# Starting the operands of the attention-weighted sums on 16-byte multiples, and taking half a batch's softmax sums from the exp instruction, in a clustered-attention and spatial-gating kernel

## The chip, the cores and the metric

The kernel runs on one core of a Trainium2 chip. Times are microseconds (us) of one execution on the device. The engines are named as the profile names them: PE (matrix multiply) with PEld (its loading of the stationary operand), DVE (vector), ACT (scalar), POOL (GpSimd) and SP, which here only issues DMAs.

## The reference

Four batches of eight heads, 768 positions, head dimension 64. Queries and keys only see each other where they fall to the same of 16 centroids.

```
q_assign = argmax(q_n @ c_n, axis=-1);  k_assign = argmax(k_n @ c_n, axis=-1)
mask = q_assign[:, :, :, None] == k_assign[:, :, None, :]
scores = where(mask, scale * q @ k.T, -1e9)
attn = exp(scores - max(scores));  attn = attn / (sum(attn) + 1e-9)
x = attn @ v                                  # then (B, S, H*D)
h = maximum(x @ w_in, 0);  u, v = h[..., :512], h[..., 512:]
v_n = (v - mean(v)) / sqrt(var(v) + 1e-6)
out = (u * (w_spatial @ v_n + b_spatial)) @ w_out
```

## The kernel before

Every fp32 operand of a large product is split into two fp16 parts, a high one and a low one; a product is three matmuls (high by high, high by low, low by high). Work is counted in pairs of heads, `n` from 0 to 15 (four pairs to a batch), and in units of one head, `(n, part)`. A sequence is `NT` = 6 blocks of 128 positions.

`prep(n)` loads and splits a pair, assigns clusters and fills `vhl`, the tile of the values: for each block `k` and head `h` a row of 64 high columns, one column of ones (column 64), one spare column and 64 low columns (`vh.t[:, k, h, 0:D + 1]` and `vh.t[:, k, h, D + 2:]`), 130 fp16 columns in all. `shifts(u)` finds an upper bound of each query's scores: PE products at L759, each reduced by DVE at L765 out of one of four PSUM buffers called `acc`, so that PE gets a buffer back when DVE has read it.

`attend(u)` has two forms. For twelve pairs keys stand on partitions: for each key block `k` scores by PE (L862, L864), exp on ACT (L872), high part on ACT (L876), low part on POOL (L877), and then the weighted sums on PE (L882): 18 matmuls, for each of six query blocks `j` one of 65 columns with the high values and the ones, one of 64 columns with the low values, one of 65 columns with the low weights. The column of ones makes the sum of the weights, so one head's result is 65 columns per query block in one `acc` buffer: `av.t[:, j * (D + 1):...]`. At `k` = 0 six more matmuls of 65 columns add a mean term. For the pairs in `ROWS` (9, 11, 13, 15, `attend_rows`) queries stand on partitions: the maximum by DVE (L820), exp (L823), high part (L825), low part (L826), a DMA transpose, and the same 18 matmuls per query block (L831), so that each exp instruction there holds the whole row of weights of 128 queries. `results` (L917 to L921) divides by the sums and writes the input of the second half.

`mlp(b)` is the second half for a batch, all in matmuls of 512 columns at L948. Its groups of six matmuls are put between the attention work of later batches; those of the last batch come at the end.

The order in which the program issues everything is written out by hand: `ORDER` is a list of the 3,164 numbers of the operations, in which the numbers are counted as the code creates them. Each engine works through its own operations in that order. A buffer of `acc` or `wk` is given, in that order, to the next who asks, the longest free one first.

## Time and profile before

| | us |
|---|---|
| median of 3 runs | 637.48 |
| lowest, highest | 636.87, 639.26 |
| the profiled execution | 635.84 |
| its span, first to last instruction | 634.1 |
| PE busy in it | 605.9 (96%) |
| DVE, ACT, POOL busy | 475.4, 439.0, 435.2 |

The profiled execution took 1.74 us more than its span, and 1.64 us less than the median. "Busy" of PE counts each matmul to its modelled end, so that overlapping matmuls are one stretch; how fast matmuls follow each other is read from the starts of rows in the timeline.

### The profile page before, as it was taken

The numbers are of one execution on the slowest core, as the hardware profiler recorded it, in microseconds if no ns is written. First come the engines' busy times: TensorE is split into PE (matmuls) and PEld (weight loads), VectorE is DVE, ScalarE is ACT, GpSimd is POOL, SyncE is SP. The second block draws the span as 40 slices with busy tenths as digits, with TensorE's granted clock in tenths as the row PEclk, the third lists the DMA queues.
The fourth block names the chain that finished last, engine by engine and source line by source line (L and its number), as shares of the span: only waits on it lengthen the run. The fifth ranks groups of instructions, "written<-read, shape, count | busy, mean of one in ns | idle before, by whom it ended". The sixth has DMA issues, their size and how long they took to land.

```text
span 634.1 us, 16399 instructions
## 1 busy us (share of the span) xinstructions
PE 605.9 (96%) x6573; PEld 363.6 (57%) x6573; DVE 475.4 (75%) x994; ACT 439.0 (69%) x674; POOL 435.2 (69%) x309
## 2 busy tenths in 40 slices
PE   3889999989999999999999999999999999999997
PEld 2537666666666667556555575575556655544443
DVE  7899999999999996877959678669798475143120
ACT  6768999999978889566477787878669964121102
POOL 2456889999789799566667787678769977223120
PEclk9969999999999999999999999999999999999999
DMA  6467865875565576728989779988996199513115
GB/s 211 135 171 162 170 150 134 174 181 147 125 154 112 115 172 97 146 67 161 180 144 192 181 126 182 184 166 144 166 167 123 38 151 154 113 22 101 33 30 153
DMA packets 174812, 87.73 MB, mean 138 GB/s; under 512 B 158448, under 2 KB 161552, under 8 KB 174736
## 3 DMA queue, kind: packets, MB, share of 16 engines
q1 hardware_dynamic: 171136, 80.40, 62.7%
q10 hardware_dynamic: 3600, 6.30, 2.9%
q8 instruction: 51, 0.84, 0.6%
q14 instruction: 25, 0.20, 0.1%
HBM read 27.63 MB, written 6.29 MB: 53 GB/s over the span
## 4 chain that ended last, share of the span: by engine, by line
PE 69%; DVE 17%; POOL 4%; DMA 4%; issue 3%; ACT 1%; SPq 0%; ACTq 0%; DVEq 0%; POOLq 0%
PE acc L948 39%; PE acc L882 7%; DVE nm L765 7%; PE acc L759 5%; PE sc L862 4%; PE sc L864 4%; PE acc L831 4%; POOL wk L877 3%; PE sc L817 2%; PE sc L815 2%; DMA wk<-wk 1%; DVE vhl L541 1%; DVE nq L820 1%; DVE wk L988 1%; DMA oht<-ohx 1%
## 5 line engine op out<-in xcount | busy, mean ns | idle before, releaser
L877 POOL TENSOR_TENSOR wk<-wk,wk 128x768 f16<-128x768 f32 x144 | 245.7, 1730 | 48.9 <-ACT wk L876 36.0
L765 DVE TENSOR_REDUCE nm<-acc 128x1 f32<-128x512 f32 (+1 forms) x216 | 138.8, 681 | 13.8 <-PE acc L759 12.7
L872 ACT ACTIVATE wk<-sc,plog 128x768 f32<-128x768 f32 x144 | 126.7, 899 | 24.0 <-PE sc L864 17.9
L948 PE MATMUL acc<-win,xT 128*128 128x512 f16 x576 | 134.9, 379 | 1.0 <-DVE u L1009 0.7
L876 ACT CAST wk<-wk 128x768 f16<-128x768 f32 x144 | 116.6, 829 | 5.5 <-PE acc L882 2.8
L948 PE MATMUL acc<-vn,wsp 128*128 128x512 f16 x432 | 101.2, 379 | 0.0
L826 POOL TENSOR_TENSOR wk<-wk,wk 128x768 f16<-128x768 f32 x48 | 80.1, 1678 | 26.2 <-ACT wk L825 24.1
L882 PEld LDWEIGHTS <-wk 128*128 128x128 f16 x2592 | 89.8, 97 | 12.0 <-POOL wk L877 1.6
L882 PE MATMUL acc<-vhl,wk 128*128 128x65 f16 (+1 forms) x2592 | 95.0, 193 | 1.3 <-POOL wk L877 1.3
L948 PEld LDWEIGHTS <-xT 128*128 128x128 f16 x576 | 55.0, 97 | 62.6 <-issue 1.5
L759 PE MATMUL acc<-hq 80*128 80x512 f16 (+1 forms) x288 | 78.6, 347 | 8.8 <-DVE nm L765 4.0
L862 PE MATMUL sc<-hq,lo 128*128 128x512 f16 (+1 forms) x288 | 72.4, 333 | 1.0 <-ACT wk L872 0.7
L864 PE MATMUL sc<-hq 81*128 81x512 f16 (+1 forms) x288 | 72.3, 332 | 0.0
L948 PE MATMUL acc<-wou,wk 128*128 128x512 f16 x288 | 67.2, 379 | 0.0
L948 PEld LDWEIGHTS <-wsp 128*128 128x128 f16 x432 | 41.2, 97 | 45.2 <-issue 0.2
L823 ACT ACTIVATE wk<-sc,nq 128x768 f32<-128x768 f32 x48 | 47.2, 990 | 26.0 <-DVE nq L822 21.4
L820 DVE TENSOR_REDUCE nq<-sc 128x1 f32<-128x768 f32 x48 | 45.6, 951 | 23.2 <-PE sc L817 18.9
L1011 POOL TENSOR_TENSOR wk<-u,wk 128x512 f16<-128x512 f32 x24 | 29.0, 1216 | 48.4 <-DVE wk L1010 28.5
L1009 DVE SCALAR_TENSOR_TENSOR u<-acc,bsp,u 128x512 f32<-128x512 f32 x24 | 17.9, 747 | 54.5 <-PE acc L948 54.5
L1019 ACT ACTIVATE wk<-acc 128x512 f32<-128x512 f32 x24 | 13.9, 595 | 46.9 <-PE acc L948 44.3
L948 PEld LDWEIGHTS <-wk 128*128 128x128 f16 x288 | 27.9, 97 | 32.2 <-issue 0.2
L759 PEld LDWEIGHTS <-hq 80*128 80x128 f16 x288 | 27.0, 101 | 31.9 <-issue 17.3
(143 smaller groups left out, 884.7 us busy)
## 6 DMA issues: line engine op xcount, KB each, us to landing
raw<-in_kqT_dram SPq DMA_DIRECT2D x15, 768.0 KB
wk<-in_vp_dram SPq DMA_DIRECT2D x16, 384.0 KB
out_dram<-wk ACTq DMA_DIRECT2D x24, 256.0 KB
hq<-hq SPq DMA_DIRECT2D x15, 384.0 KB
hq<-lo SPq DMA_DIRECT2D x15, 192.0 KB
lo<-hq SPq DMA_DIRECT2D x15, 192.0 KB
wraw<-in_wsT_dram SPq DMA_DIRECT2D x12, 192.0 KB
vn<-in_w_in_dram SPq DMA_DIRECT2D x4, 512.0 KB
```

The lines of the kernel that those rows point to most:

```text
L759: T.matmul(out=acc.t[:, i * w:(i + 1) * w], lhsT=hq.t[0:R_SH, 1, h, t * P:(t + 1) * P], rhs=hq.t[0:R_SH, 0, h, cs], start=i == 0, stop=i = ...
L765: V.tensor_reduce(out=cols(nm.t), in_=src, axis=AX.X, op=ALU.max, negate=True)
L820: o = op("DVE", lambda sc=sc, nq=nq: V.tensor_reduce(out=nq.t[:, 0:1], in_=sc.t[:, 0:S], axis=AX.X, op=ALU.max, negate=True), after=[o], u ...
L823: o = op("ACT", lambda sc=sc, p32=p32, nq=nq: A.activation(out=p32.t, in_=sc.t[:, 0:S], func=AF.Exp, bias=nq.t[:, 2:3], scale=nq.t[:, 1:2] ...
L826: o = op("POOL", lambda pt=pt, p32=p32: G_.tensor_tensor(out=pt.t[:, 1, :], in0=p32.t, in1=pt.t[:, 0, :], op=ALU.subtract), after=[o], use ...
L862: T.matmul(out=sc.t[:, c:c + cs.stop - cs.start], lhsT=lo.t[:, h, ks], rhs=hq.t[:, 2, h, cs], start=True, stop=False)
L864: T.matmul(out=sc.t[:, c:c + cs.stop - cs.start], lhsT=hq.t[0:R_E, 0, h, ks], rhs=hq.t[0:R_E, 1, h, cs], start=False, stop=True)
L872: A.activation(out=p32.t, in_=sc.t[:, 0:S], func=AF.Exp, bias=plog, scale=SC_UNIT)
L876: o = op("ACT", lambda pt=pt, p32=p32: A.copy(out=pt.t[:, 0, :], in_=p32.t), after=[o], use=[p32], new=[pt])
L877: o = op("POOL", lambda pt=pt, p32=p32: G_.tensor_tensor(out=pt.t[:, 1, :], in0=p32.t, in1=pt.t[:, 0, :], op=ALU.subtract), after=[o], use ...
L882: T.matmul(out=av.t[:, j * (D + 1):j * (D + 1) + w], lhsT=lhsT, rhs=rhs, skip_group_check=True, **f)
L948: T.matmul(out=acc.t, lhsT=lr[m][0], rhs=lr[m][1], start=(m == 0), stop=(m == n - 1))
```

## The change

The row of `vhl` grows from 130 to 136 columns (272 bytes), with the low values from column 72 on; a query block's result in `acc` takes 68 columns (272 bytes) and not 65. The small tiles `wh` and `wl` now share one. In `attend_rows` exp gives the sum of each row as a second output (`accum_out`) into a new small tile `rs`, the three matmuls per block have 64 columns each, and `results` reads `rs` where it read column 64 of `acc`. The other twelve pairs keep the column of ones. `ORDER` is another list of the same 3,164 numbers; no engine has more or fewer instructions.

```diff
+LO, V_COLS, AV_COLS = 72, 136, 68
 ORDER = [
...
-    vhl = [const.tile([P, NT, 2, 2 * D + 2], F16, name="vhl%d" % i) for i in range(V_BUFS)]
+    vhl = [const.tile([P, NT, 2, V_COLS], F16, name="vhl%d" % i) for i in range(V_BUFS)]
...
-    whs = [const.tile([2, 2, D + 2], F16, name="wh%d" % i) for i in range(2)]
-    wls = [const.tile([2, 2, D + 2], F16, name="wl%d" % i) for i in range(2)]
+    whl = [const.tile([34, 2, D + 2], F16, name="whl%d" % i) for i in range(2)]
+    whs = [x[0:2] for x in whl]
+    wls = [x[32:34] for x in whl]
...
+    r_rs = R(sm, "rs", [P, NT], F32, 2)
...
# attend_rows
-            o = op("ACT", lambda sc=sc, p32=p32, nq=nq: A.activation(out=p32.t, in_=sc.t[:, 0:S], func=AF.Exp, bias=nq.t[:, 2:3], scale=nq.t[:, 1:2]), after=[o], use=[sc, nq], new=[p32])
+            o = op("ACT", lambda sc=sc, p32=p32, nq=nq, t=t: A.activation(out=p32.t, in_=sc.t[:, 0:S], func=AF.Exp, bias=nq.t[:, 2:3], scale=nq.t[:, 1:2], accum_out=rs.t[:, t:t + 1]), after=[o], use=[sc, nq] + ([rs] if t else []), new=[p32] + ([] if t else [rs]))
...
-                    T.matmul(out=av.t[:, t * (D + 1):t * (D + 1) + w], lhsT=lhsT, rhs=rhs, skip_group_check=True, **f)
+                    T.matmul(out=av.t[:, t * AV_COLS:t * AV_COLS + w], lhsT=lhsT, rhs=rhs, skip_group_check=True, **f)
                 for k in range(NT):
-                    mm(D + 1, ptT.t[:, k], vh.t[:, k, h, 0:D + 1], start=t == 0 and k == 0, stop=False)
-                    mm(D, ptT.t[:, k], vh.t[:, k, h, D + 2:], start=False, stop=False)
-                    mm(D + 1, ptT.t[:, NT + k], vh.t[:, k, h, 0:D + 1], start=False, stop=t == NT - 1 and k == NT - 1)
+                    mm(D, ptT.t[:, k], vh.t[:, k, h, 0:D], start=t == 0 and k == 0, stop=False)
+                    mm(D, ptT.t[:, k], vh.t[:, k, h, LO:], start=False, stop=False)
+                    mm(D, ptT.t[:, NT + k], vh.t[:, k, h, 0:D], start=False, stop=t == NT - 1 and k == NT - 1)
...
# attend
                     mm(j, D + 1, pt.t[:, 0, js], vh.t[:, k, h, 0:D + 1], start=False, stop=False)
-                    mm(j, D, pt.t[:, 0, js], vh.t[:, k, h, D + 2:], start=False, stop=False)
+                    mm(j, D, pt.t[:, 0, js], vh.t[:, k, h, LO:], start=False, stop=False)
                     mm(j, D + 1, pt.t[:, 1, js], vh.t[:, k, h, 0:D + 1], start=False, stop=stop)
...
# results
-        a = op("DVE", lambda: V.tensor_scalar(out=rc.t, in0=avv()[:, :, D], scalar1=f, scalar2=1e-9 * 2.0 ** P_LOG * f, op0=ALU.mult, op1=ALU.add), after=[prev], use=[av], new=[rc])
+        a = op("DVE", lambda: V.tensor_scalar(out=rc.t, in0=rs.t if rs else avv()[:, :, D], scalar1=f, scalar2=1e-9 * 2.0 ** P_LOG * f, op0=ALU.mult, op1=ALU.add), after=[prev], use=[rs or av], new=[rc])
```

The new list moves operations by a few places nearly everywhere. Two places follow as the built programs have them; line numbers of the changed kernel are three higher than those of the kernel before.

The first is the start of the first batch's second half. On PE of the kernel before, the last scores ahead of it and its first matmul, which stands 3,389 rows into PE's list:

```order
L864 LDWEIGHTS hq
L864 MATMUL sc_127<-hq 128x512
L864 LDWEIGHTS hq
L864 MATMUL sc_127<-hq 128x256
L948 LDWEIGHTS xT_104
L948 MATMUL acc_128<-win,xT_104 128x512 [waits DVE_49]
```

In the changed kernel that matmul stands 3,409 rows in, behind weighted sums:

```order
L885 LDWEIGHTS wk_119
L885 MATMUL acc_128<-vhl_89,wk_119 128x64
L885 LDWEIGHTS wk_119
L885 MATMUL acc_128<-vhl_89,wk_119 128x65
L951 LDWEIGHTS xT_102
L951 MATMUL acc_129<-win,xT_102 128x512 [waits DVE_49]
```

It waits for an `acc` buffer that DVE has to read first. On DVE of the kernel before, the seven instructions up to the one that frees it (281 on DVE's list):

```order
L765 TENSOR_REDUCE nm_91<-acc_128 128x1
L765 TENSOR_REDUCE nm_91<-acc_131 128x1 [waits PE_49]
L776 TENSOR_REDUCE nl<-nm_92 128x6 [waits DVE_49]
L541 SCALAR_TENSOR_TENSOR vhl_90<-wk_109,vhl_90 128x12x64 [waits DMAHW0_49,Activation_49]
L486 TENSOR_SCALAR acc_130<-wou 128x512 [waits DMAHW1_49]
L471 SCALAR_TENSOR_TENSOR wsp<-wraw_124,wsp 128x384 [waits DMAHW3_49]
L765 TENSOR_REDUCE nm_92<-acc_128 128x1 [waits DVE_49,PE_49]
```

On DVE of the changed kernel, the seven up to the one that frees it there (280 on the list):

```order
L768 TENSOR_REDUCE nm_91<-acc_128 128x1 [waits PE_49]
L768 TENSOR_REDUCE nm_92<-acc_126 128x1 [waits DVE_49,PE_49]
L768 TENSOR_REDUCE nm_91<-acc_129 128x1
L768 TENSOR_REDUCE nm_92<-acc_126 128x2 [waits PE_49]
L768 TENSOR_REDUCE nm_91<-acc_128 128x1
L474 SCALAR_TENSOR_TENSOR wsp<-wraw_122,wsp 128x384 [waits DMAHW1_49]
L768 TENSOR_REDUCE nm_91<-acc_129 128x2 [waits PE_49]
```

The same kinds of work stand ahead in both: PE has 20 rows (ten matmuls with their loads) more ahead of the second half, DVE one row fewer.

The second place is on PE at the first weighted sums of a pair in `ROWS`. Before:

```order
L817 LDWEIGHTS hq
L817 MATMUL sc_127<-hq 128x256
L831 LDWEIGHTS wk_113 [waits DMAHW5_49]
L831 MATMUL acc_130<-vhl_90,wk_113 128x65 [waits Activation_49]
L831 LDWEIGHTS wk_113
L831 MATMUL acc_130<-vhl_90,wk_113 128x64
```

After, where a group of the second half stands ahead:

```order
L951 LDWEIGHTS xT_103
L951 MATMUL acc_126<-win,xT_103 128x512
L834 LDWEIGHTS wk_110 [waits DMAHW1_49]
L834 MATMUL acc_128<-vhl_90,wk_110 128x64 [waits Activation_49]
L834 LDWEIGHTS wk_110
L834 MATMUL acc_128<-vhl_90,wk_110 128x64
```

The number of matmuls and of loads is the same; 576 matmuls lose one column.

## Rows read from the trace of the kernel before

**Rows 1.** The page, parts 1 and 2: busy time of PE (share of the span, instructions), and the granted PE clock in 40 slices of 15.9 us, in tenths.

```profile
PE 605.9 (96%) x6573; PEld 363.6 (57%) x6573; DVE 475.4 (75%) x994; ACT 439.0 (69%) x674; POOL 435.2 (69%) x309
...
PEclk9969999999999999999999999999999999999999
```

**Rows 2.** Busy time by stretch of the span: from:to, length, then busy us and instructions of each engine, granted clock, DMA share, GB/s.

```profile
0.00:60.00 60.00, 44.90 (x417) 25.69 (x418) 54.38 (x137) 42.17 (x66) 28.75 (x34) 0.86 0.63 172
60.00:140.00 80.00, 74.20 (x1208) 53.77 (x1207) 78.19 (x154) 78.78 (x128) 74.45 (x49) 1.00 0.74 162
140.00:216.00 76.00, 74.08 (x972) 49.19 (x972) 73.26 (x147) 68.48 (x114) 64.72 (x43) 1.00 0.57 133
216.00:634.00 418.00, 412.74 (x3979) 234.96 (x3977) 269.55 (x559) 249.57 (x370) 267.32 (x186) 1.00 0.67 130
```

**Rows 3.** What PE waited for between 60 and 216 us: waiting line, whom for, us in total, times, longest.

```profile
PE acc L759 <- DVE nm L765: 3.3, 6, 1.0
PE acc L882 <- POOL wk L877: 1.3, 2, 1.0
PE acc L759 <- DMA hq<-oht: 0.9, 1, 0.9
```

**Rows 4.** The same between 216 and 634 us (two of four rows; the others are 0.2 us each).

```profile
PE acc L948 <- DVE u L1009: 0.7, 1, 0.7
PE acc L831 <- DMA wk<-wk: 0.4, 1, 0.4
```

**Rows 5.** The weighted sums of L882 by stretch: from:to, length, PE busy (number of matmuls), PEld busy, clock, DMA share, GB/s.

```profile
0.00:140.00 140.00, 33.76 (x912) 32.09 (x912) 0.94 0.69 166
140.00:216.00 76.00, 21.11 (x570) 20.28 (x570) 1.00 0.57 133
216.00:634.00 418.00, 44.49 (x1254) 43.13 (x1254) 1.00 0.67 130
```

**Rows 6.** The weighted sums of L831 (pairs in `ROWS`) in the last stretch; they have none in the others.

```profile
216.00:634.00 418.00, 32.88 (x864) 31.58 (x864) 1.00 0.67 130
```

**Rows 7.** PE's timeline at two long runs of weighted sums: start, us to the modelled end, line, number. The row behind each run shows where the next matmul starts.

```profile
239.52 3.47 PE L882 MATMUL acc<-vhl,wk 128*128 128x65 f16 x108
242.82 0.49 PE L862 MATMUL sc<-hq,lo 128*128 128x512 f16 x2
...
453.22 1.82 PE L831 MATMUL acc<-vhl,wk 128*128 128x65 f16 x54
454.87 0.49 PE L815 MATMUL sc<-lo,hq 128*128 128x512 f16 x2
```

**Rows 8.** PE's timeline in unit (4, 1), `h` = 1: the groups of 18 for key blocks `k` = 1, 2 and 5, each with the row that follows it.

```profile
157.08 0.70 PE L882 MATMUL acc<-vhl,wk 128*128 128x65 f16 x18
157.62 0.60 PE L759 MATMUL acc<-hq 80*128 80x256 f16 x3
...
158.93 0.71 PE L882 MATMUL acc<-vhl,wk 128*128 128x65 f16 x18
159.48 0.38 PE L759 MATMUL acc<-hq 80*128 80x512 f16 x1
...
163.74 0.70 PE L882 MATMUL acc<-vhl,wk 128*128 128x65 f16 x18
164.28 0.38 PE L759 MATMUL acc<-hq 80*128 80x256 f16 x2
```

**Rows 9.** PE's timeline at 24 matmuls of cluster logits, 64 and 32 columns by turns (L641, L642; first row and the row that follows the last), whose operands all start on multiples of 16 bytes.

```profile
228.60 0.19 PE L641 MATMUL sc<-cmx,hq 128*128 128x64 f16 x1
...
229.26 0.49 PE L862 MATMUL sc<-hq,lo 128*128 128x512 f16 x2
```

**Rows 10.** Groups of instructions: line, engine, operation, out<-in, shapes, number | busy us, mean ns | idle before, whom for.

```profile
L823 ACT ACTIVATE wk<-sc,nq 128x768 f32<-128x768 f32 x48 | 47.2, 990 | 26.0 <-DVE nq L822 21.4 <-issue 2.1 <-POOL wk L826 1.9
L872 ACT ACTIVATE wk<-sc,plog 128x768 f32<-128x768 f32 x144 | 126.7, 899 | 24.0 <-PE sc L864 17.9 <-DMA wk<-wk 3.2 <-POOL wk L877 2.3
L782 ACT ACTIVATE shx<-nl 128x6 f16<-128x6 f32 x24 | 5.5, 229 | 4.1 <-DVE nl L776 2.4 <-DMA sht<-shx 1.7
L541 DVE SCALAR_TENSOR_TENSOR lo<-raw,hq 128x768 f16<-128x768 f32 x28 | 32.4, 1166 | 3.1 <-ACT hq L613 2.8 <-ACT hq L552 0.3
L541 DVE SCALAR_TENSOR_TENSOR vhl<-wk,vhl 128x768 f16<-128x768 f32 x13 | 17.4, 1339 | 1.9 <-ACT vhl L693 1.9
```

**Rows 11.** The timeline of DVE and of PE around the start of the first batch's second half.

```profile
144.50 0.68 DVE L765 TENSOR_REDUCE nm<-acc 128x1 f32<-128x512 f32 x1
...
145.23 2.75 PE L948 MATMUL acc<-win,xT 128*128 128x512 f16 x12 [0.24 <-DVE nm L765]
```

**Rows 12.** The chain that ended last, its longest piece (start, us, what).

```profile
542.30 85.48 PE acc L948 x396
```

More of the change, by code (lines that the diff above doesn't have):

```diff
@@ L367 @@
     r_vhl = R(None, "vhl", None, None, V_BUFS, tiles=vhl)
-    r_vhl0 = R(None, "vhl0", None, None, 2, tiles=[wspf[:, 1560 * i:1560 * (i + 1)].rearrange("p (t h c) -> p t h c", t=NT, h=2) for i in range(2)])
+    r_vhl0 = R(None, "vhl0", None, None, 2, tiles=[wspf[:, 2 * NT * V_COLS * i:2 * NT * V_COLS * (i + 1)].rearrange("p (t h c) -> p t h c", t=NT, h=2) for i in range(2)])
     scratch = r_wk.new()
@@ L693, in values @@
         o_vh = op("ACT", lambda: A.activation(out=vh.t[:, :, :, 0:D], in_=vraw.t.rearrange("p t (h d) -> p t h d", d=D), func=AF.Copy, scale=V_SCALE), after=[ldv, c_one], use=[vraw], new=[vh])
-        o_vl = low(n, 2, lambda: vh.t[:, :, :, D + 2:], lambda: vraw.t.rearrange("p t (h d) -> p t h d", d=D), lambda: vh.t[:, :, :, 0:D], V_SCALE, [o_vh], [vraw, vh], [])
+        o_vl = low(n, 2, lambda: vh.t[:, :, :, LO:], lambda: vraw.t.rearrange("p t (h d) -> p t h d", d=D), lambda: vh.t[:, :, :, 0:D], V_SCALE, [o_vh], [vraw, vh], [])
         if n in ROWS:
@@ L704, in sums @@
                 T.matmul(out=o[:, :, 0:D + 1], lhsT=ones, rhs=vh.t[:, t, :, 0:D + 1], start=(t == 0), stop=False, skip_group_check=True)
-                T.matmul(out=o[:, :, 0:D], lhsT=ones, rhs=vh.t[:, t, :, D + 2:], start=False, stop=(t == NT - 1), skip_group_check=True)
+                T.matmul(out=o[:, :, 0:D], lhsT=ones, rhs=vh.t[:, t, :, LO:], start=False, stop=(t == NT - 1), skip_group_check=True)
         short = n >= 2 * NPR
@@ L806, in attend_rows @@
         hq, lo, vh = X["hq"], X["lo"], X["vhl"]
-        av = r_acc.new()
+        av, rs = r_acc.new(), r_rs.new()
         prev = None
@@ L830, in mm @@
                 def mm(w, lhsT, rhs, **f):
-                    T.matmul(out=av.t[:, t * (D + 1):t * (D + 1) + w], lhsT=lhsT, rhs=rhs, skip_group_check=True, **f)
+                    T.matmul(out=av.t[:, t * AV_COLS:t * AV_COLS + w], lhsT=lhsT, rhs=rhs, skip_group_check=True, **f)
                 for k in range(NT):
-                    mm(D + 1, ptT.t[:, k], vh.t[:, k, h, 0:D + 1], start=t == 0 and k == 0, stop=False)
-                    mm(D, ptT.t[:, k], vh.t[:, k, h, D + 2:], start=False, stop=False)
-                    mm(D + 1, ptT.t[:, NT + k], vh.t[:, k, h, 0:D + 1], start=False, stop=t == NT - 1 and k == NT - 1)
+                    mm(D, ptT.t[:, k], vh.t[:, k, h, 0:D], start=t == 0 and k == 0, stop=False)
+                    mm(D, ptT.t[:, k], vh.t[:, k, h, LO:], start=False, stop=False)
+                    mm(D, ptT.t[:, NT + k], vh.t[:, k, h, 0:D], start=False, stop=t == NT - 1 and k == NT - 1)
             prev = op("PE", values, after=[o, prev] + X["v"], use=[ptT, vh] + ([av] if t else []), new=[] if t else [av])
-        results(u, av, prev)
+        results(u, av, prev, rs)
     def attend(u):
@@ L881, in mm @@
                 def mm(j, w, lhsT, rhs, **f):
-                    T.matmul(out=av.t[:, j * (D + 1):j * (D + 1) + w], lhsT=lhsT, rhs=rhs, skip_group_check=True, **f)
+                    T.matmul(out=av.t[:, j * AV_COLS:j * AV_COLS + w], lhsT=lhsT, rhs=rhs, skip_group_check=True, **f)
                 for j, (h, t) in enumerate(u.blocks):
@@ L895, in attend, with results @@
         results(u, av, prev)
-    def results(u, av, prev):
+    def results(u, av, prev, rs=None):
         b, p = divmod(u.n, NPR)
@@ L906, in avv @@
         def avv():
-            return av.t[:, 0:NT * (D + 1)].rearrange("p (t c) -> p t c", c=D + 1)
+            return av.t[:, 0:NT * AV_COLS].rearrange("p (t c) -> p t c", c=AV_COLS)
         def dst(i):
```

264 rows, old and new, of the table ORDER are left out of this document.

## The prediction

> **What bounds the kernel now.** I read the page's busy times first, then the span in four stretches, then what PE waited for in each. PE is busy for 605.9 of 634.1 us, the other engines for 475 and less [rows 1]. The stretches tell when that holds. Up to 60 us PE has 44.9 us of work and DVE 54.4; the clock granted to PE is 0.86 on average and lowest in the third slice [rows 1, 2]. From 60 to 140 us DVE is busy for 78.2 of 80 us and ACT for 78.8: PE can only have what they hand over. From 140 to 216 us PE has 74.1 of 76 us and DVE 73.3, so both matter. From 216 us on PE has 412.7 of 418 us and DVE only 269.6 [rows 2].
>
> The waits agree. Up to 216 us the longest sum is PE waiting for DVE to read an `acc` buffer, 3.3 us in six waits [rows 3]; behind 216 us the two largest are single waits of 0.7 and 0.4 us [rows 4]. At the end the chain is one piece of 85.5 us of PE, 396 matmuls [rows 12]. So what PE is spared after 216 us should come off the time, what it is spared before 140 us should turn into waiting for DVE, and between the two I count half.
>
> **The weighted sums on PE.** Busy time doesn't price a matmul here, because matmuls overlap; the distance of starts does. In one run of 108 it is (242.82 - 239.52) / 108 = 30.6 ns, in one of 54 at L831 (454.87 - 453.22) / 54 = 30.6 ns [rows 7]. All attention-weighted sums cost that: 2,736 at L882, of which 912 up to 140 us, 570 from there to 216 us and 1,254 after it [rows 5], and 864 at L831, all after 216 us [rows 6].
>
> What would they cost with aligned operands? Three rows bound it. The stretch of 396 wide matmuls takes 215.9 ns for each, 2.5 ns over 512 columns at 2.4 GHz [rows 12]; with 65 and 64 columns that makes 29.6 and 29.2 ns, on average 29.5. The logits with 64 and 32 columns by turns, on 16-byte multiples, take (229.26 - 228.60) / 24 = 27.5 ns [rows 9]; that is a floor, as half of them are narrow. The third is a comparison inside the old kernel. Row (k, h) of `vhl` starts at byte 260 (2k + h), its low part 132 bytes behind, so the low part lies on a multiple of 16 only for h = 1 and odd k. In unit (4, 1) the groups k = 1 and k = 5 took 0.54 us to the next start, the group k = 2 0.55 us [rows 8]. The step of these rows is 0.01 us, so this is faint, but it says that aligning a third of the operands is worth about 10 ns in 550. Three thirds, if they pay alike, give 520 / 18 = 28.9 ns. I take 29.2 ns at L882, between 28.9 and 29.5, and 28.8 at L831, where two matmuls in three also lose a column (0.4 ns each at 2.4 GHz, rounded up). The ends are no gain at all (30.6) and 27.5.
>
> TensorE: Matmul & The Clock Gate, in the section "Wait — 56ns, not 53.3ns?" of the Trainium skill, gives the distance of starts as columns by 2.4 GHz plus about 2.5 ns, without a term for where an operand begins; by it only the lost columns would pay, 576 times 0.4 ns, some 0.2 us. The wide matmuls agree with it; the 30.6 ns of the weighted sums do not.
>
> **The sum.** After 216 us: 1,254 x 1.4 = 1.8 us at L882 and 864 x 1.8 = 1.6 us at L831. From 140 to 216 us: 570 x 1.4 = 0.8, half of it 0.4. Before: 912 x 1.4 = 1.3, which I count as nothing, because DVE, at 98%, covers it; without that cover it would come on top. Together 3.7 us. At 27.5 ns the same places give 3.9 + 2.7 + 0.9 = 7.5 us; at 30.6 nothing.
>
> **The sum of a row from exp.** The 48 exps at L823 take 990 ns, those at L872 without scales per partition 899 [rows 10]. No instruction of the trace has a second output. I take 0.1 us more for each, as the scales cost; the ends are nothing and the 229 ns of a whole small ACT instruction at L782 [rows 10]. 0.1 x 48 = 4.8 us on ACT, which after 216 us is busy for 249.6 of 418 us [rows 2]. Behind a late exp stand the high part, the low part on POOL, the transpose and the sums of that block; PE has groups of the second half to put there, and waited only once for a transpose, 0.4 us [rows 4]. So I count it at nothing; without that cover it is 0.1 us per block, up to 4.8. The division reads its sums from SBUF and no longer waits for PE to do so; the product behind it still does. Nothing.
>
> **Writes of values and of results.** The thirteen splits of values on DVE take 1,339 ns where the contiguous splits of keys take 1,166 [rows 10]; if their output's new start gave them the difference, that is 2.2 us of DVE over the whole span, and only a part of it falls where DVE decides. I count it at nothing. The shared tile for `wh` and `wl` and the wider steps in `acc` move no instruction.
>
> **The list.** It could matter more than all that: DVE's order sets when PE gets buffers, up to 216 us. The start of the second half is where the two lists can be compared: before, the matmul there waits 0.24 us for a reduce on DVE that ends at 145.2 us [rows 11], instruction 281 of DVE's list; now it waits for instruction 280, of the same kinds, and PE has ten matmuls more ahead of it. I take the new list as neutral, with an uncertainty of 3 us to either side, about the 3.3 us of one kind of wait that PE has between 60 and 216 us [rows 3].
>
> The profiled execution took 635.84 us; 635.8 - 3.7 = 632.1. It lies 1.6 us under the median of the runs, so the forecast for the median is **633.8 us**, 0.6% less. 0.5% (3.2 us) is about what a measurement of this kernel can tell from no change.
>
> **Rivals.**
>
> *Only operands that lose a line gain.* SBUF — State Buffer, in the Specifications of the Trainium skill, names lines of 16 bytes and a penalty for each crossing; no row shows the lines themselves. As a mechanism: 64 columns are 128 bytes, eight pieces of 16 from an aligned start and nine from any other, but 65 columns are nine from either. Then a third of L882 gains, the 10 ns in 18 of [rows 8], and only L831 all of it. That is 0.7 us after 216 us (1,254 / 18 x 10 ns), 0.2 between, and 48 x 30 ns = 1.4 us at L831: 2.3 us, 635.2 us, within 0.5%. For it speaks that just the low parts are aligned in the groups that took 0.54; against it nothing that rows of this step could show.
>
> *An operand's start costs nothing.* If the 30.6 ns have another cause, only the 576 lost columns count, 0.2 us, and the time is 637.3. The TensorE section named above would have it so. Against it: the 0.01 us between the groups of [rows 8], and no other cause that the rows show.
>
> *The list spares PE waiting.* If half of the 5.5 us in [rows 3] and some of the idle 15 us before 60 us go (60 - 44.9 [rows 2]), 4 us more come off: 629.8. For it: DVE is 98% full only from 60 us on. Against it: the same kinds of work stand ahead of the second half.
>
> *The list costs waits.* If in the new places PE's waits between 60 and 216 us double, 5.5 us more [rows 3], and the start loses another 1.5, the time is 640.8. It decides from 3.7 + 3.2 = 6.9 us of new waits on. For it: the list moved everywhere, and this stretch has no slack on DVE. Against it: the row by row likeness at the start of the second half.
>
> **Chances.** The forecast, 630.5 to 636: 0.50, of which 0.35 is faster by over 0.5%. Only lost lines pay: 0.12, within. Nothing pays: 0.08, within. The list spares waits: 0.15, faster. The list costs waits: 0.15, half of it slower by over 0.5%. That makes 0.50 faster, 0.42 within 0.5%, 0.08 slower. The range of 629.5 to 638.5 leaves out the lower part of the third case and most of the fourth, under two in ten.
>
> **What would show it.** The distance of starts in runs of weighted sums: 29.2 ns and 28.8 expected; 30 or more at L882 beside 29 at L831 would be the first rival. PE's waits between 60 and 216 us: some 1 us longer, since DVE hasn't become faster; much more or less is the list. The exps with a second output: 1.0 to 1.2 us. The wrong step would most likely be the list, or the half I count from 140 to 216 us.

## The result, and the profile after

The changed kernel takes 641.95 us in the median of 6 runs (640.72 to 643.55), beside 637.36 us of the kernel before in the same comparison: 1.007 times as long, 95% interval 1.0046 to 1.0094. In a second comparison (e18) it took 640.8 us (7 runs) beside 637.16, 1.006 (1.0036 to 1.0084), where one slow run of the kernel before, of 1,578 us, is left out of the ratio. So it is 0.6 to 0.7% slower. 633.8 had been forecast; the result lies above the range.

The profiled execution took 643.21 us with a span of 641.4, 7.3 more than before. Its page, parts 1 and 2 [rows 1 before]:

```profile
PE 609.4 (95%) x6573; PEld 363.3 (57%) x6573; DVE 478.9 (75%) x994; ACT 446.6 (70%) x722; POOL 432.8 (67%) x309
...
PEclk9956999999999999999999999999999999999999
```

ACT has 48 instructions more than before (722 for 674), so the sentence of the section on the change that no engine has more is wrong. The granted clock is lower in the third slice and above all in the fourth (48 to 64 us). The stretches [rows 2 before]:

```profile
0.00:60.00 60.00, 44.03 (x313) 23.71 (x314) 50.93 (x131) 38.83 (x59) 25.44 (x32) 0.77 0.63 160
60.00:140.00 80.00, 71.98 (x1179) 51.83 (x1178) 75.92 (x145) 77.11 (x123) 70.53 (x46) 1.00 0.71 148
140.00:216.00 76.00, 75.21 (x1008) 49.77 (x1006) 72.59 (x148) 69.04 (x115) 64.27 (x43) 1.00 0.62 148
216.00:641.00 425.00, 418.16 (x4082) 237.94 (x4078) 279.43 (x572) 261.66 (x428) 272.60 (x191) 1.00 0.66 129
```

In the first 60 us PE was busy nearly as long as before (44.0 us for 44.9), but started only 313 matmuls instead of 417, at a granted clock of 0.77 instead of 0.86: a part of the time is lost there. (In the profiled run of e18, the same kernel again, it was 385 matmuls at 0.80.) What PE waited for from 60 to 216 us [rows 3 before]:

```profile
PE acc L762 <- DVE nm L768: 2.9, 9, 1.0
PE acc L762 <- DMA hq<-oht: 1.3, 1, 1.3
PE acc L762 <- DVE ohx L677: 1.3, 1, 1.3
PE sc L865 <- ACT wk L875: 1.2, 2, 0.9
PE acc L707 <- DVE nm L768: 0.6, 1, 0.6
PE acc L885 <- DVE nm L768: 0.5, 2, 0.4
```

With 0.2 us of a smaller row that makes 8.0 us. [rows 3] are only the three largest rows of the kernel before, 5.5 us; with three more of 0.2 us and the one below it waited 6.8 us:

```profile
PE sc L862 <- ACT wk L872: 0.7, 2, 0.6
```

In e18 the sum is 7.0. So these waits grew by 1.2 us or by 0.2, and most of the loss isn't in them. The start of the first batch's second half, and the long piece of the chain at the end [rows 11, 12 before]:

```profile
152.03 1.24 PE L951 MATMUL acc<-win,xT 128*128 128x512 f16 x5
...
549.67 85.48 PE acc L951 x396
```

The second half starts at 152.0 us, before at 145.2: 6.8 of the 7.3 us are lost by then. From there to the end of the span it is 641.4 - 152.0 = 489.4 us now and 634.1 - 145.2 = 488.9 before. In these two executions the slowdown is wholly a matter of the first 150 us. And what the change should have brought behind them isn't there either.

Weighted sums, the new exp and the division in the changed kernel, PE's timeline first [rows 7, 10 before]:

```profile
150.95 1.25 PE L885 MATMUL acc<-vhl,wk 128*128 128x65 f16 x36
152.03 1.24 PE L951 MATMUL acc<-win,xT 128*128 128x512 f16 x5
...
459.74 0.69 PE L834 MATMUL acc<-vhl,wk 128*128 128x64 f16 x18
460.26 0.49 PE L818 MATMUL sc<-lo,hq 128*128 128x512 f16 x2
```

```profile
L826 ACT ACTIVATE wk<-sc,nq 128x768 f32<-128x768 f32 x48 | 47.5, 990 | 24.6 <-DVE nq L825 5.8 <-DVE nq L824 4.7 <-DMA xT<-wk 4.0
L544 DVE SCALAR_TENSOR_TENSOR vhl<-wk,vhl 128x768 f16<-128x768 f32 x13 | 17.6, 1353 | 0.0
L826 ACT ACTIVATION_READ_ACCUMULATOR wk<-sc,nq 128x1 f32 x48 | 9.3, 194 | 0.0
L920 DVE TENSOR_SCALAR rc<-rs 128x6 f32<-128x6 f32 x8 | 6.4, 806 | 0.0
L920 DVE TENSOR_SCALAR rc<-acc 128x6 f32<-128x6 f32 x24 | 3.8, 157 | 3.6 <-PE acc L885 3.5
```

A sum of L885 stands (152.03 - 150.95) / 36 = 30.0 ns from the next (30.6 before), one of L834 (460.26 - 459.74) / 18 = 28.9 (30.6 before).

### The profile page after: what moved, and what is told of

The parts are those of the page before. It is cut to its first block, busy times and chain, and to the rows that moved or that the text cites. A ratio compares the mean times of both kernels' runs of the same rounds, so it can differ in the third digit from the quotient of the medians.

```text
span 641.4 us, 16489 instructions
## 1 busy us (share of the span) xinstructions
PE 609.4 (95%) x6573; PEld 363.3 (57%) x6573; DVE 478.9 (75%) x994; ACT 446.6 (70%) x722; POOL 432.8 (67%) x309
## 4 chain that ended last, share of the span: by engine, by line
PE 72%; DVE 14%; ACT 4%; DMA 3%; issue 3%; POOL 1%; SPq 1%; ACTq 0%; DVEq 0%
PE acc L951 39%; PE acc L885 8%; PE acc L762 6%; DVE nm L768 5%; PE sc L865 5%; PE sc L867 5%; PE acc L834 4%; PE sc L818 2%; PE sc L820 2%; DMA xT<-wk 2%; DVE lo L544 1%; ACT wk L879 1%; DMA raw<-in_kqT_dram 1%; POOL wk L880 1%; ACT wk L875 1%
## 5 line engine op out<-in xcount | busy, mean ns | idle before, releaser
L768 DVE TENSOR_REDUCE nm<-acc 128x1 f32<-128x512 f32 (+1 forms) x216 | 140.4, 681 | 25.3 <-PE acc L762 25.0
L951 PE MATMUL acc<-vn,wsp 128*128 128x512 f16 x432 | 99.6, 379 | 1.0 <-DVE nm L768 0.9
L885 PEld LDWEIGHTS <-wk 128*128 128x128 f16 x2592 | 90.1, 98 | 10.9 <-issue 1.1
L885 PE MATMUL acc<-vhl,wk 128*128 128x65 f16 (+1 forms) x2592 | 95.4, 194 | 0.2 <-POOL wk L880 0.2
L762 PE MATMUL acc<-hq 80*128 80x512 f16 (+1 forms) x288 | 82.4, 360 | 11.7 <-DVE nm L768 3.8
L823 DVE TENSOR_REDUCE nq<-sc 128x1 f32<-128x768 f32 x48 | 45.8, 954 | 28.8 <-PE sc L820 25.4
L993 POOL TENSOR_TENSOR vn<-wk,vn 128x512 f16<-128x512 f32 x24 | 29.6, 1239 | 24.8 <-DVE vn L992 24.4
```

What stands on the lines that cost most here:

```text
L762: T.matmul(out=acc.t[:, i * w:(i + 1) * w], lhsT=hq.t[0:R_SH, 1, h, t * P:(t + 1) * P], rhs=hq.t[0:R_SH, 0, h, cs], start=i == 0, stop=i = ...
L768: V.tensor_reduce(out=cols(nm.t), in_=src, axis=AX.X, op=ALU.max, negate=True)
L823: o = op("DVE", lambda sc=sc, nq=nq: V.tensor_reduce(out=nq.t[:, 0:1], in_=sc.t[:, 0:S], axis=AX.X, op=ALU.max, negate=True), after=[o], u ...
L885: T.matmul(out=av.t[:, j * AV_COLS:j * AV_COLS + w], lhsT=lhsT, rhs=rhs, skip_group_check=True, **f)
L951: T.matmul(out=acc.t, lhsT=lr[m][0], rhs=lr[m][1], start=(m == 0), stop=(m == n - 1))
```

## The experiments

All ran beside the kernel before, whose medians there were 636.4 to 637.4 us. "Old" and "new" is the list. The clock is the mean over the runs of a kernel; "start" is the first matmul of the first batch's second half in the profiled run, "rest" the span behind it.

```
kernel                              list us      ratio [95%]              clock  start  rest
before                              old  637.2   1                        0.987  145.2  488.9
changed                             new  641.95  1.0070 [1.0046, 1.0094]  0.980  152.0  489.4
e18 changed again                   new  640.8   1.0060 [1.0036, 1.0084]  0.981  149.8  488.6
e1  change's code                   old  635.5   0.9977 [0.9964, 0.9990]  0.986  145.8  488.1
e17 the same again                  old  636.1   0.9988 [0.9968, 1.0008]  0.985  145.1  486.4
e15 starts alone                    old  637.3   1.0007 [0.9991, 1.0023]  0.986  145.8  488.3
e16 exp's sums alone                old  636.6   1.0005 [0.9988, 1.0022]  0.987  147.8  488.9
e8  sums 65 apart                   old  636.7   0.9991 [0.9982, 1.0001]  0.987  146.6  488.4
e13 sums 66 wide                    old  636.2   0.9997 [0.9977, 1.0016]  0.986  146.1  488.5
e2  code of before                  new  639.9   1.0044 [1.0029, 1.0060]  0.980  149.4  488.1
e3  old head, then new              -    646.0   1.0136 [1.0119, 1.0153]  0.982  155.0  489.4
e4  products twice                  new  652.0   1.0225 [1.0209, 1.0240]  0.972  161.7  488.6
e5  128 rows, wider transfers       new  650.9   1.0226 [1.0195, 1.0257]  0.983  159.9  489.8
e6  128 rows, wider transfers       old  647.9   1.0167 [1.0138, 1.0196]  0.986  155.8  490.1
e7  products halved                 new  639.5   1.0039 [1.0016, 1.0061]  0.980  148.6  488.7
e9  128 rows                        new  639.5   1.0039 [1.0021, 1.0056]  0.991  148.1  488.9
e10 128 rows                        old  636.6   0.9990 [0.9965, 1.0015]  0.989  147.9  489.1
e11 one load first                  new  640.0   1.0073 [1.0041, 1.0105]  0.982  152.8  488.6
e12 pair 3 early                    new  643.4   1.0114 [1.0079, 1.0148]  0.977  152.5  488.6
e14 128 rows and pair 3 early       new  642.6   1.0114 [1.0071, 1.0158]  0.987  150.6  489.2
```

The last column hardly moves: whatever was edited, it stays between 486.4 and 490.1 us, and without e17 between 488.1 and 490.1. The start carries most of the differences.

### Code and list apart

e1 is the changed kernel with the list of the kernel before, e2 the kernel before with the new list. (In kernels with the old list and the new code, line numbers are 47 higher than in the kernel before: L929 is its L882.)

```diff
 ORDER = [
-...the new list
+...the list of the kernel before          # e1; e2 the other way round, on the old code
```

> The changed code with the list of before. Theory L (the list is what loses, by leaving PE's clock at the lower level for 27 us of the first 60 where the kernel before had 17): 634 to 636 us, the first batch's second half starts at 145 us as before, the lower clock ends at about 50 us, and the new operands are worth 1.5 to 3 us. Rival C (the code loses: unaligned pieces elsewhere, the second output of exp, the 806 ns division input): 640 us or more with this list too.

Measured: 635.49 us beside 637.41. Once more, as e17:

> The change's code with the old list once more, in the same comparison as its two halves, since its first time rests on 6 runs: 635.5 us if that stands, some 636.5 us if the other kernels that differ from it little (636.2 and 636.7 us) show the true size.

Measured: 636.08 us beside 636.94. So the code alone gains 0.9 to 1.9 us; the second interval includes no gain.

> The code of before with the new list. Theory L: 642 to 645 us, the second half of the first batch starts at about 152 us and the lower clock lasts to about 59 us. Rival C: 636 to 638 us.

Measured: 639.94 us, 1.0044 of the kernel before, 2.8 us more (2.5 by the medians). The list alone makes the kernel slower. 1.0044 times 0.9977 (e1) or 0.9988 (e17) makes 1.002 or 1.003; the changed kernel is at 1.006 and 1.007, 1.8 to 3.1 us more than that (e18's interval begins at 1.0036):

> The changed kernel itself once more, as its 641.95 us rest on 6 runs that fall into two groups (640.8 and 643.2 us). Theory A+ (the change's code makes the new list's stretch at the lower clock longer still, so that list and code together cost more than one by one): again 641 to 643 us, a clock of 0.980 in the mean, 1.006 to 1.008 of the kernel before. Theory E (list and code simply add up, +2.8 and -0.9 us): 638.5 to 640 us, 1.003 to 1.004.

Measured: 640.8 us, 1.0060, nearer to A+ than to E. The profile of e2 shows less of what the changed one shows, at the same place: its second half starts at 149.4 us, and PE ran at the lower clock for 20.5 of the first 60 us (before 17.1, changed 27.3, e18 23.9).

e3 took the list of before up to the second half's first operation and the new one from there:

```diff
 ORDER = [
-...the new list
+...the first 915 of the list of before, then the rest as the new list has them
```

> The changed code; the list of before up to the first matmul of the first batch's second half, and behind it the operations that are left in the order of the new list. Theory L, with the loss all in the head of the list: 634 to 636.5 us, like the changed code with the old list. If the rest of the new list loses too: 638 to 642.

Measured: 646.04 us (1.0136). It tells nothing on the rest of the list, since the seam itself cost more than either: from 140 to 216 us PE had only 68.1 us of work in this stretch.

```profile
140.00:216.00 76.00, 68.14 (x822) 43.05 (x820) 64.26 (x127) 60.43 (x100) 54.66 (x37) 0.96 0.49 120
```

### What is lost before 60 us

Three kernels from 48 to 60 us, in stretches of 4: before, changed, and e9 (below). Columns as in [rows 2].

```profile
48.00:52.00 4.00, 4.00 (x20) 2.02 (x19) 3.91 (x8) 3.04 (x7) 0.00 (x0) 0.81 0.49 105
52.00:56.00 4.00, 3.91 (x89) 3.11 (x87) 4.00 (x8) 4.00 (x8) 3.96 (x3) 1.00 0.67 173
56.00:60.00 4.00, 4.00 (x72) 3.04 (x71) 3.93 (x8) 2.28 (x4) 4.00 (x3) 1.00 1.06 256
```

```profile
48.00:52.00 4.00, 4.00 (x13) 1.76 (x12) 3.42 (x8) 2.87 (x6) 1.22 (x1) 0.50 0.66 179
52.00:56.00 4.00, 4.00 (x18) 1.82 (x17) 3.07 (x6) 2.27 (x4) 0.00 (x0) 0.50 0.84 159
56.00:60.00 4.00, 4.00 (x50) 3.14 (x48) 3.31 (x5) 2.11 (x4) 2.85 (x2) 0.59 0.76 193
```

```profile
48.00:52.00 4.00, 3.09 (x16) 1.38 (x15) 3.97 (x10) 2.39 (x7) 0.89 (x1) 1.00 0.56 160
52.00:56.00 4.00, 3.94 (x59) 2.73 (x58) 4.00 (x7) 4.00 (x6) 0.85 (x1) 1.00 0.98 197
56.00:60.00 4.00, 4.00 (x102) 3.51 (x101) 3.93 (x8) 4.00 (x8) 4.00 (x3) 1.00 0.74 230
```

Before, PE is back at 2.4 GHz at 49.5 us, and DVE is full throughout. In the changed kernel PE works without a pause but at 1.2 GHz until 59.3 us (a granted clock of 0.50), and DVE, which was the bound, has 9.8 us of work in 12 and waits for PE. The means over the runs agree: with the new list and these products as they were the clock is 0.977 to 0.982 (e11, e12 below included), with the old list 0.985 to 0.987. 0.980 of 640 us is 2 x 0.020 x 640 = 26 us at the lower level, 0.987 is 17: 9 us more, which cost PE half of that, some 4.5 us of work. How much time that is, is another question. What it was doing there, from 40 to 60 us, changed kernel:

```profile
L762 PE MATMUL acc<-hq 80*128 80x512 f16 x16 | 8.3, 622 | 0.0
L762 PE MATMUL acc<-hq 80*128 80x256 f16 x16 | 4.8, 402 | 0.1
L865 PE MATMUL sc<-hq,lo 128*128 128x512 f16 x5 | 2.9, 581 | 0.0
```

Mostly the products of the shifts, whose operands fill 80 of 128 rows. e4 asked first whether more work on PE would bring the clock back:

```diff
-                for i, (j, cs) in enumerate(parts):
+                for i, (j, cs) in enumerate(parts * 2 if u.n in (1, 2) else parts):
+                    i %= m
```

> The changed kernel, but each score product of the upper bound of pairs 1 and 2 (72 matmuls) is issued twice into the same buffer, so that PE has more to do between 38 and 60 us while it waits for DVE; the second overwrites the first. Theory L with the clock as the means: the lower clock ends earlier than at 59 us (about 50), and the time falls by 2 to 4 us to 638 to 640 in spite of some 15 us more of work on PE at the lower clock or 8 at the full. If the clock is only an accompaniment of a list that hands PE too little work: the time grows by 1 to 8 us.

Measured: 652.0 us, and in the profiled run the lower clock lasted from 36.9 to 67.7 us. So more of these products don't raise it, and PE at the lower clock is the bound there: up to the start of the second half PE is busy for 138.1 us instead of 128.0, 10.2 more, and the time is 10.1 us longer. Then the same products over all rows, and cut into more instructions:

```diff
-                    T.matmul(..., lhsT=hq.t[0:R_SH, 1, h, ...], rhs=hq.t[0:R_SH, 0, h, cs], ...)
+                    T.matmul(..., lhsT=hq.t[0:128, 1, h, ...], rhs=hq.t[0:128, 0, h, cs], ...)   # rows 80 to 127 of the first are zero
-            m = C if x > 1 else C + 1
+            m = C + 3 if x > 1 else C + 1          # e5 and e6 only: zeros for rows 80 to 82 with the marks
```

> The changed kernel, but the key-by-query products of the shifts (line L762) of all pairs except those in the first of the four hq buffers run over 128 rows of the array instead of 80: rows 80 to 127 of one operand are zero, so the sums are the same and the number of instructions and columns too. Theory A (what keeps TensorE at the lower clock from 32 to 59 us is that it runs almost nothing but these products there, which fill only 80 of 128 rows): the lower clock ends at 46 to 50 us instead of 59, some 10 us at double speed sooner, so the end comes 3 to 5 us earlier, 637 to 639 us. Theory B (the clock follows the idle time before, the hole at 36 to 39 us, and not the rows): still some 27 us at the lower clock and 641 to 643 us.

> The change's code with the old list (e1_new_code_old_list, 635.5 us), with the same products over 128 rows. Theory A: the second low stretch, 38.9 to 49.2 us there, ends at 42 to 46 us, which gives back 2 to 3 us: 632.5 to 633.5 us. Theory B: 635.5 us and 17 us at the lower clock, as without.

Measured: 650.92 and 647.88 us, both far slower. At the lower clock the profiled runs were before 60 us for 13.7 us (e5) and 6.8 us (e6), instead of 27.3 and 17.1; but PE waited 12.5 us for the marks in e5, where the changed kernel had 3.6 from 30 to 150 us:

```profile
PE acc L770 <- DMA hq<-oht: 12.5, 6, 4.7
```

Two things had come with the edit: 28.5 instead of 24 KB in two transfers of each pair, and a fill with zeros of 2.1 us on POOL ahead of pair 1's splits. e9 and e10 leave the transfers as they were, put the fill into a gap of POOL and widen only pairs 1 to 3:

```diff
-        rows_in = P if n % HQ_BUFS else R_SH
-            m = C + 3 if x > 1 else C + 1
+        rows_in = P if 0 < n < HQ_BUFS else R_SH
+            m = C if x > 1 else C + 1
```

> The changed kernel, but the shifts' products of pairs 1 to 3 alone run over 128 rows of the array (48 rows more, zero on one side), with the transfers of the marks as they are in the changed kernel: in e5 these carried three rows more, TensorE waited for them 12.5 us instead of 3.6 us, and that hid what the rows did. Theory A (the clock stays low from 32 to 59 us because TensorE runs little but products over 80 rows there): some 10 to 17 us at the lower clock instead of 27, as e5 showed it, and 3 to 5 us less time than the changed kernel's 641.95: 637 to 639 us. Theory B (the rows raise the clock but the time is not lost through the clock): the low stretch is shorter and the time stays at 641 to 643 us.

> The same edit on the change's code with the old list (635.5 us, 17 us at the lower clock). Theory A: 7 to 10 us at the lower clock and 2 to 4 us less: 631.5 to 633.5 us, below both kernels. Theory B: 635 to 636 us.

Measured: e9 639.54 us, with a mean clock of 0.991, 10.2 us at the lower one in the profiled run. PE had started 414 matmuls by 60 us, nearly the 417 of the kernel before; the second half starts at 148.1 us. So the clock comes back earlier in all three new-list kernels with 128 rows (e5, e9 and e14 below), and with it PE's work of the first 60 us. In time that is 1.3 us (against e18) to 2.4 us by the medians, 1.3 to 2.0 by the ratios, and the intervals overlap. e10: 636.56 us, no gain over the same kernel without the edit (635.5, 636.1). There PE came back at 41.9 us, waited for DVE twice between 50.1 and 51.9 us (0.3 and 1.2 us), and from 52.1 us the clock was low once more, for 3.4 us.

```diff
-                top([(i, halves[0])], lambda x, i=i: x[:, i, 0:1])
+                top([(i, slice(0, 256)), (i, slice(256, 512))] if n in (1, 2) else [(i, halves[0])], ...)
```

> The changed kernel, but each 512-column product of the shifts of pairs 1 and 2 is written as two of 256 columns: the same columns over 80 rows, a third more instructions there. Theory C (the clock looks at how many instructions come): a shorter stretch at the lower clock than 27 us and 638 to 640 us. Theories A and B: as the changed kernel, about 27 us and 641 to 643 us.

Measured: 639.48 us, with a mean clock of 0.980. Theory C falls as far as the clock goes: more instructions over 80 rows didn't raise it over the runs. But the time is as good as e9's, by a way that I can't name; against e18 the difference is inside the intervals.

How much of the loss is the clock? The stretch up to the start of the second half answers that, in the kernel before, the changed one, e2 and e9 (columns as in [rows 2]):

```profile
0.00:145.23 145.23, 124.07 (x1694) 83.09 (x1695) 137.80 (x298) 126.18 (x200) 107.46 (x85) 0.94 0.68 163
0.00:152.03 152.03, 127.96 (x1704) 84.61 (x1705) 138.05 (x298) 127.93 (x201) 107.17 (x84) 0.91 0.68 156
0.00:149.40 149.40, 127.05 (x1705) 84.59 (x1705) 137.98 (x298) 127.19 (x202) 106.92 (x84) 0.93 0.69 159
0.00:148.14 148.14, 121.41 (x1705) 81.38 (x1706) 137.90 (x298) 127.94 (x202) 109.42 (x87) 0.97 0.70 160
```

DVE is the fullest engine there: 298 instructions and 138 us in each. What differs is how long it stands idle: 7.4 us before, 14.0 in the changed kernel (12.2 in e18), 11.4 in e2 and 10.2 in e9. PE in e9 has 2.7 us less work than in the kernel before, as its clock is higher, but stands idle for 5.6 us more. So with a better clock than before e9 still starts 2.9 us later and takes 1.0039, 2.5 us more: the rows give back 1.3 to 2.0 us of 3.8 to 4.5, and the larger part of the loss is still there when the clock is mended. The runs of the kernel before agree. Beside the experiments there are 105 of them; the ten with a mean clock of 0.982 or less took 637.1 us on average, the 39 with 0.988 or more 637.1 too (where in those runs the lower clock lay isn't on record).

### What is lost from 60 to 150 us

The waits of e9 from 60 to 216 us, whose clock is better than that of the kernel before:

```profile
PE acc L764 <- DVE nm L770: 2.9, 9, 1.0
PE acc L764 <- DVE ohx L678: 1.3, 1, 1.3
PE acc L764 <- DMA hq<-oht: 1.2, 1, 1.2
PE acc L708 <- DVE nm L770: 1.0, 1, 1.0
```

With the smaller rows they make 8.1 us, and they are those of the changed kernel, so they belong to the list and not to the clock. I suspected pair 3, which the new list prepares later: on SP its load stands behind a transpose that waits.

```profile
35.55 0.58 SPq L609 DMA_DIRECT2D raw<-in_kqT_dram  x1
38.91 2.06 SPq L676 DMA_TRANSPOSE oht<-ohx  x1
```

```profile
38.55 1.26 SPq L679 DMA_TRANSPOSE oht<-ohx  x1
39.91 0.53 SPq L612 DMA_DIRECT2D raw<-in_kqT_dram  x1
```

(before, then changed). e11 moves the load alone, e12 the load and pair 3's next steps, e14 adds the rows of e9:

```diff
 # SP        -transpose of pair 2's marks, load of pair 3      +load of pair 3, transpose          (e11, e12, e14)
 # ACT       pair 3's two copies ahead of the copy that waits for L792's product                   (e12, e14)
 # DVE       pair 3's two low parts behind the reductions of pair 1                                (e12, e14)
 # PE        pair 3's logits ahead of the fourth scores of unit (0, 1)                             (e12, e14)
```

> The changed kernel with one operation of its list moved: on SP the load of pair 3's raw keys and queries (raw<-in_kqT, issued at 39.9 us) goes ahead of the transpose of pair 2's marks that waits until 38.5 us; in the kernel before it stood there (35.6 us). Theory D (the list loses through pair 3, whose preparation it starts later): the load lands some 4 us earlier. If that alone decides, 638 to 640 us. If the places of the next steps on ScalarE and VectorE bind (their copy at 48.0 us stands behind one that waits for TensorE until 46.9 us), at most 0.5 us: 641 to 642.5 us. Theory A (the clock alone): no change, 641 to 643 us.

> The same move and those behind it: ScalarE's two copies of pair 3's operands ahead of the copy that waits until 46.9 us, VectorE's two low parts of them behind the reductions of pair 1 (as in the list before, 48 and 51 us, instead of 55.7 and 56.6 us), and TensorE's logits of pair 3 two steps earlier. Theory D: the marks of pair 3 come 3 to 5 us earlier, TensorE's waits for them at 83 to 93 us go, and the time falls by 2 to 3 us to 639 to 640 us. Theory A: the low stretch of the clock stays 24 to 27 us long and the time 641 to 643 us.

> The changed kernel with the moves of e12 and the products of pairs 1 to 3 over 128 rows as in e9 (639.5 us, 10 us at the lower clock). Theories A and D together (the clock and pair 3 are the whole loss of the list): 635.5 to 637 us, as the change's code with the old list. If either is not a cause: 639 to 640 us.

Measured: 639.99, 643.42 and 642.6 us. Theory D falls. The load was issued at 36.9 us in e11, and the copy of it still began at 47.7 (48.0 in the changed kernel). In its profiled run PE was at the lower clock for 17.1 of the first 60 us, as in the kernel before, and the second half yet started at 152.8. In e12 the low parts came at 48.6 and 51.0, near those of the kernel before (47.8 and 50.7), and the second half started no sooner (152.5). In e14 the clock was up from 47.0 us on and PE then stood idle, with 1.55 us of work from 48 to 52:

```profile
48.00:52.00 4.00, 1.55 (x6) 0.46 (x5) 4.00 (x8) 1.51 (x4) 0.60 (x1) 1.00 0.92 247
```

DVE was full there: 1.9 us of low parts between its reductions held back the buffers that PE wanted. None of the three moves by itself gave time back; which places of the list lose it stays open.

### The code's own gain

e15 and e16 take it apart, with the old list:

```diff
# e15, attend_rows and results as in the kernel before; the new starts stay
-                    mm(D, ptT.t[:, k], vh.t[:, k, h, 0:D], ...)
+                    mm(D + 1, ptT.t[:, k], vh.t[:, k, h, 0:D + 1], ...)
# e16, exp's sums stay
-LO, V_COLS, AV_COLS = 72, 136, 68
+LO, V_COLS, AV_COLS = 66, 130, 65
```

> The kernel before with the new starts alone (V's low part at column 72 of 136, outputs 68 apart) and the old list; exp gives no sums, the weighted sums of the heads with queries on partitions stay 65 wide where they were. By the spacing of e1's rows 18 sums of the main kind take 545 ns instead of 554, 144 groups give 1.3 us; of the other kind about 537 instead of 549 ns, 48 groups give 0.6 us: 1.9 us less than the kernel before, 635.4 us. Rival: the starts give nothing that lasts, since other engines set the end of what TensorE shortens: 637.3 us.

> The kernel before with exp's sums alone (48 more read-outs of 194 ns on ScalarE, 8 divisions' inputs of 685 ns instead of 156 on VectorE, two of three of those weighted sums 64 wide instead of 65) and the old starts and the old list. A column is 0.4 ns, so 12 x 48 of them give 0.2 us of TensorE, and the two additions lie on engines that are not the bound after 216 us: 637.1 us. Rival: the added work on the way from scores to weighted sums costs: 637.5 to 638.5 us.

Measured: 637.27 and 636.6 us beside 636.94; no difference for either.

The distances of starts, averaged in the profiled runs over all weighted sums of the twelve pairs (the line that was L882) that follow each other directly at the full clock, in ns, by the place in the three of a query block:

```
                        high values  low values  low weights   all
                        even  odd    even  odd   even  odd
before                  30.3  29.2   31.8  31.8  29.3  30.2    30.5
changed                 33.5  30.8   28.4  28.7  29.2  29.2    30.0
e1                      33.4  30.8   28.6  28.6  29.2  29.2    30.0
e8, outputs 65 apart    34.0  29.9   28.9  29.1  29.2  29.8    30.2
e13, 66 columns         33.1  31.1   28.5  28.7  29.2  29.2    30.0
e15, starts alone       33.4  30.6   28.6  28.7  29.3  29.1    30.0
e16, exp's sums alone   30.3  29.3   31.9  31.7  29.3  30.2    30.5
```

The aligned low part became 3 ns faster, as forecast, and on even query blocks the matmul ahead of it became 3 ns longer to the next start. Two reasons that I could think of were tried, the output's place and the odd width:

```diff
-LO, V_COLS, AV_COLS = 72, 136, 68
+LO, V_COLS, AV_COLS = 72, 136, 65                                        # e8
-                    mm(j, D + 1, pt.t[:, 0, js], vh.t[:, k, h, 0:D + 1], ...)
+                    mm(j, D + 2, pt.t[:, 0, js], vh.t[:, k, h, 0:D + 2], ...)   # e13, the low weights too
```

> The change's code with the old list (635.5 us), but the weighted sums of a unit stand 65 words apart in PSUM again, not 68; the operands from V keep their new starts. If the place of the output is what slowed the first 65-column sum of each three (from 29.5 to 33 to 35 ns on even query blocks), these go back to 29.5 ns, 18 weighted sums take some 530 ns instead of 547, and 69 times 6 or more such groups give 1 to 1.2 us: 634.4 us. If it isn't, the spacing stays and the time is 635.5 us.

> The change's code with the old list (635.5 us), but the weighted sums that were 65 columns wide are 66 wide (one column more, which nobody reads, filled with ones). If it is the odd width that holds back the aligned sum behind it (33 to 35 ns on every second query block instead of 29.5), the spacing becomes 29 ns throughout, 18 sums take some 528 ns instead of 545, and 144 such groups give 2 us: 633 to 634 us. If it isn't, each of the 12 wide sums costs 0.4 ns more and the time is 635.5 to 636.5 us.

Measured: 636.7 and 636.21 us, and the 33 to 34 ns stayed in both. Why even blocks are held back is open. At the line that was L831, 18 sums take 549 ns before, 541 in e15, 540 in e16 and 526 in e1 with both. The distances there show what e13 could not: the sum with the high values of even key blocks is followed after 32.9 ns in e15, with 65 columns, and after 29.6 in e1, with 64. So there the longer distance goes with the 65th column, and a 66th doesn't cure it.

## Why the prediction was wrong

**The step that failed: "I take the new list as neutral".** It rested on one place, the start of the second half, where the same kinds of work stood ahead in both lists. That is a likeness of what stands there, and says nothing of when it is reached: the start moved by 6.8 us in the profiled run, and by 4.2 with the code of before (e2). The uncertainty of 3 us to either side was about right for the list alone (2.8) and too small for the changed kernel. Of the 8.2 us between the forecast and the median, 2.8 are the list alone and 1.7 to 2.7 the gain that is missing with the old list (0.9 to 1.9 for 3.6); the rest came only with list and code together, and its cause stays open.

**The rival "The list costs waits", 640.8 us, had the time, but hardly by its mechanism.** It had 5.5 us more of PE's waits between 60 and 216 us and 1.5 at the start. Measured were 1.2 more (8.0 for 6.8), in e18 0.2, about the 1 us that the prediction itself gave as the sign of no loss by the list. What grew is PE's time at the lower clock before 60 us (27.3 for 17.1 us in the profiled run, 23.9 in e18, about 5 and 3 us of PE's work), and DVE's waiting for PE. The clock was in front of me, 0.86 in [rows 2] and a third slice of 6 in [rows 1], and I passed over the first 60 us as DVE's, where PE's idle time covers all; [rows 3] don't even show them. At half the clock PE is the bound there, 12.00 us of work from 48 to 60 us, and DVE waits, 9.8 us of work. That e9's rows go with a shorter stretch is shown; that the longer stretch is the larger part of the loss is not: e9 keeps 2.5 us of it at a better clock, and there PE waits instead. Why the order makes them wait, and why code and order together lose 1.8 to 3.1 us more than one by one, stays open.

**The gain of 1.8 us at L882 was mis-sized.** 29.2 ns were taken, 30.0 measured: (30.5 - 30.0) x 1,254 = 0.6 us. The reading of [rows 8], that aligning a third gives 10 ns in 550, was right for the whole: all thirds together give (30.5 - 30.0) x 18 = 9 ns. The multiplication by three was wrong. The first rival ("Only operands that lose a line gain") had that size. The low part fell from 31.8 ns to 28.6 with the new starts (e15; 28.9 to 29.1 with the old places of the output, e8), and the 65-column sums gained nothing together. SBUF — State Buffer, in the section "Specifications (TRN2)" of the Trainium skill, names lines of 16 bytes and a penalty for each crossing; that only the low part gained agrees with it, that a neighbour paid for it on every second block is not in it. TensorE: Matmul & The Clock Gate, in the section "Wait — 56ns, not 53.3ns?" of the Trainium skill, has no term for the start; the 3 ns of the low part differ from it, and the measurement decides.

**The gain of 1.6 us at L831 was nearly right.** 28.8 ns were taken, 526 / 18 = 29.2 measured, 48 x (549 - 526) = 1.1 us.

**That what PE is spared after 216 us comes off the time was only partly right.** With the old list PE was busy 411.2 us behind 216 us in e1 for 412.7, 1.6 us less as the rows say. But PE's waits there grew from 1.5 us [rows 4] to 2.9 in e1 (2.5 in e17):

```profile
PE acc L995 <- DVE wou L518: 1.2, 1, 1.2
PE acc L806 <- DVE nm L812: 0.8, 1, 0.8
PE acc L806 <- DVE xn L966: 0.6, 1, 0.6
PE acc L878 <- DMA wk<-wk: 0.3, 1, 0.3
```

In e1 nearly all that PE was spared there came back as waiting for DVE; the whole rest of the span was 0.8 us shorter in e1 and 2.5 in e17.

**Exp's second output** is an instruction of its own of 194 ns behind each exp, whose 990 ns didn't change; 0.1 us was taken, 0.229 was the bound. That it lies under cover was right as far as e16 can tell. **Its division input** cost 806 ns and not nothing (157 from `acc`). The values' split gained nothing from its new start (1,353 ns for 1,339), as counted.

The list of things that would show it had the distances right: 30 or more at L882 beside 29 at L831 was named as the sign of the first rival, and it is what the rows show. It had no sign for the first 60 us, where the loss begins.

## What to carry to other kernels

A new order of operations is not neutral because the same work stands ahead of a landmark in it; where PE runs at its lower clock early in a kernel, look at what decides there first, since half the clock turns PE into the bound of a stretch in which it looks covered. Time one half of a change with the other half of the kernel before, code and order apart: here that took two runs, and showed that the order cost 2.8 us and the code gained 0.9 to 1.9. And take a suspected cause away before calling it the cause: with the clock mended (e9) PE waited instead, and most of the loss was still there. The code with the old list (e1, e17) is the fastest seen, 0.1 to 0.2% under the kernel before, in e17 within the interval.
